# Splitting the flag's step: the minimum on VectorE first, TensorE's matmul four tiles later

## The chip, the cores and the metric

The kernel runs on one core of one Trainium2 chip. Its time is device time in microseconds (us). Three runs of the kernel before took 269.99, 271.73 and 272.43 us, so the median is 271.73; the execution in the profile took 270.14 us, of which the span from the first to the last instruction is 268.4 us.

## What is computed

Four batches of N = 12416 rows of C = 128 numbers go through two attention steps with m = 32 inducing rows, and then through a gated layer of width 1536:

```python
def mab(q, kv):
    s = scale * (q @ kv.transpose(0, 2, 1))
    s = s - s.max(-1, keepdims=True)
    a = np.exp(s)
    a /= a.sum(-1, keepdims=True) + 1e-09
    return a @ kv
h = mab(I, x)          # 32 rows look at all of x
y = mab(x, h)          # all of x looks at the 32 rows
...
gate = np.maximum(y @ w_gate, 0.0)
val = y @ w_val
out = (gate * val) @ w_out
```

The result has 49664 rows of 128 numbers in float32.

## The kernel before

Since every row of y is a weighted mean of the same 32 rows h, gate and val are weighted means of 32 rows too, once it is known which of the gates are positive. For each batch the kernel builds a table of the products of pairs of these rows, multiplied with w_out; each output row is then a sum over pairs, with an exponential of a sum of two scores for each pair. This holds if, for each of the 1536 units, the sign of the gate is the same for all rows. The kernel bounds that from the scores it has seen. Per batch, `certain` (L432) puts what it finds into `kept` (128 x 12) and `near` (128 x 1), by a few small operations on VectorE and GpSimd. After the last batch, `flag` (L806) takes the smallest of them: a minimum over the columns of `kept` (L809), a minimum with `near` (L810), a matmul with a matrix of ones which adds up the 128 partitions on TensorE (L812), a comparison (L814) and a cast to an integer (L818). The result `left` is loaded into a register by all engines (L885), and only if it is positive a second, general kernel runs after this one. With these inputs it does not run.

The rest of the work around the flag is the output of the last batch. A batch has 97 tiles of 128 rows, numbered 0 to 96. `scores` (L558) makes a buffer of exponentials: TensorE adds pairs of scores into one of two PSUM buffers `e_ps` (L569), and ACT takes the exponential into one of 20 buffers `F` (L576). `outputs` (L583) makes one tile: four matmuls with the table (L591) and a fifth (L593) into a third of a PSUM buffer `o_ps`. There are two such buffers. After three tiles `outputs_end` (L599) lets VectorE take the reciprocal of the row sums (L607) and multiply (L608) into an output buffer; after six tiles that is sent to memory by the sync queue (L617).

Nothing is scheduled automatically. The order of instructions on every engine is the order in which the Python code emits them, and that is written by hand in the string `ORDER`: each letter is a step. E is one call of `scores`, O is one tile, and s, x, p, u, l and t take the next step of a list ("lane"). The lane s has, per batch, the scores of the next pieces of x and then the three steps of the bound; the last entry is the flag. Each engine takes its own instructions in that order and waits where an input or a buffer isn't ready.

At the end of the string the last s is the flag, behind tile 77 of the last batch. Tile 77 is the third of its group (75, 76, 77). After it stand tile 78, the last E of full size, tiles 79 to 89, the E of the last 128 columns, tiles 90 to 95, x and tile 96. The value load L885 stands after tile 88.

Of the kernel before, what the change touches and what calls it, by code (L numbers as in the profile page):

```python
# [10 lines left out]
FP32 = mybir.dt.float32  # L11
FP16 = mybir.dt.float16
AF = mybir.ActivationFunctionType
ALU = mybir.AluOpType
AX = mybir.AxisListType


def quadratic_kernel(tc, x, inducing, moe_w_gate, moe_w_val, moe_w_out, out):


    with ExitStack() as ctx:
        return quadratic_body(
            ctx, tc, x, inducing, moe_w_gate, moe_w_val, moe_w_out, out
        )


def quadratic_body(ctx, tc, x, inducing, moe_w_gate, moe_w_val, moe_w_out, out):
    nc = tc.nc
# [3 lines left out]
    P = 128  # L32
# [20 lines left out]
    def st(shape, dtype, tag, bufs, name=None, pool=None):  # L53
        return (pool or sb).tile(shape, dtype, tag=tag, bufs=bufs, name=name or tag)
# [13 lines left out]
    ones32 = constp.tile([P, P], FP32, name="ones32")  # L68
    ones16 = constp.tile([P, P], FP16, name="ones16")
    zero16 = constp.tile([1, 2 * P], FP16, name="zero16")  # L70
    kept = constp.tile([P, NFF], FP32, name="kept")
    near = constp.tile([P, 1], FP32, name="near")
# [40 lines left out]
    def mt(shape, dtype, tag, bufs, name=None):  # L113
        return st(shape, dtype, tag, bufs, name, pool=mp)
# [216 lines left out]
    def bank(tag, name, shape, dtype=FP32):  # L331
        return psum.tile(shape, dtype, tag=tag, bufs=2, name=name)
# [8 lines left out]
    dve, act, pool = nc.vector, nc.scalar, nc.gpsimd  # L341
# [318 lines left out]
    lanes = {"p": [], "u": [], "s": [], "x": [], "l": [], "t": []}  # L660
    turning = []

    def plan_scores(b):
        for q in range(0 if b else 1, NCH):
            lanes["s"].append(lambda q=q: pair_out(b, q, *pair_scores(b, q)))
            lanes["x"].append(lambda q=q: pair_exp(b, q))
        lanes["s"] += [
            lambda: bound1(b),
            lambda: (bound2(b), bound3(b)),
            lambda: certain(b),  # L670
        ]

    def plan_phase1(b):

        s = state[b]
# [127 lines left out]
        for n, g in late[::-1]:  # L803
            todo.insert(n, g)
        lanes["u"] += todo
    def flag():  # L806

        sure = mt([P, 1], FP32, "v", 1)
        dve.tensor_reduce(out=sure, in_=kept, axis=AX.X, op=ALU.min)  # L809
        dve.tensor_tensor(out=sure, in0=sure, in1=near, op=ALU.min)  # L810
        ps = bank("m", "flag_ps", [P, 1])
        nc.tensor.matmul(ps, ones32, sure, start=True, stop=True)  # L812
        f32 = mt([P, 1], FP32, "eps", 1)
        dve.tensor_scalar(  # L814
            out=f32, in0=ps, scalar1=P - 0.5, scalar2=1.0, op0=ALU.is_le, op1=ALU.mult
        )
        left = flag.left = constp.tile([P, 1], mybir.dt.int32, name="left")
        dve.tensor_copy(out=left, in_=f32)  # L818

    lanes["u"].append(lambda: gate_sum(0, 1))  # L820
    for b in range(1, B):
        plan_phase1(b)
    for b in range(B):
        plan_scores(b)
    lanes["s"].append(flag)


    def all_k(t0, nt):
# [70 lines left out]
    "OOEOOsEEOOpOOEOpEOOOuEOuuEOOEOOuEOEuOOxOOsEEOxOOOOuuEEOsOOOEuuOOEOuOExOOOuOuEEOOxsOuEsEs"  # L899
    "uOOOOEOEuuEOuOEsEEOOOOuOEEOOuuOsEOOEOuuEEOOOEOOuOEuOEuOOOuOOxEEOOOuOEEOOOOOOEEOOOOEOOOxO"  # L900
    "EEOOOOsEOEOxOOOEEOOOOEOOEOOEsEOOEOOOEsEOOxOOOEEOOOEOOOEOOExOOOOEEsOOOEOOOEsOOOEEOsOOOxsO"
    "EEOOOOEOOOOEEOOOsOEOOOOOOOOOOOEOOOOOOxO"
)


# [202 lines left out]
```

The softmax here doesn't subtract the row's maximum and nothing guards it: scores larger than these inputs give would overflow.

## Time and profile before

| what | value |
|---|---|
| median of three runs | 271.73 us |
| profiled execution, span | 268.4 us |
| TensorE busy (matmul) | 247.3 us, 92% |
| ACT busy | 227.5 us, 85% |
| VectorE busy | 214.3 us, 80% |
| GpSimd busy | 27.1 us, 10% |
| mean granted TensorE clock | 0.986 |
| HBM read and written | 27.80 and 25.43 MB |

Busy times are sums over the whole span, and several engines can be busy at once. What sets the time is read from the chain that ended last, which is followed back from the last instruction, and from the waits: who stood idle, until whose result came. In the tables of the trace, a name such as `o_ps` is the program's name of a buffer, "L591" is the line of the code, "PE" is TensorE, "PEld" its weight loads, "DVE" VectorE, "ACT" ScalarE, "POOL" GpSimd and "SP" the sync engine, which issues the output transfers. The last operation of VectorE ends at 262.56 us, and the last output transfer is issued at 262.60 us.

### The profile page before, as it was taken

What the parts mean: (1) busy time and instruction counts of PE and PEld (TensorE: products, weight loads), DVE (VectorE), ACT (ScalarE), POOL (GpSimd) and SP (SyncE); (2) the same over time, 40 slices, a digit from 0 to 9 for tenths busy, and PEclk for the clock granted to TensorE, in tenths of its full rate; (3) what the DMA queues carried; (4) which work ended last, traced back from release to release, by engine and by line L of the source; (5) the groups of instructions that cost most, each with busy time, mean ns of one, the idle gap of its engine ahead of it and who ended that gap; (6) DMA issues with size and microseconds to landing.
All of it is one profiled execution on the core that took longest, in us unless ns stands there. A gap on an engine that the chain in (4) does not pass through costs nothing.

```text
span 268.4 us, 9193 instructions
## 1 busy us (share of the span) xinstructions
PE 247.3 (92%) x3885; PEld 186.6 (70%) x3885; DVE 214.3 (80%) x584; ACT 227.5 (85%) x305; POOL 27.1 (10%) x71
## 2 busy tenths in 40 slices
PE   2996899999999999998899999999999999999890
PEld 0794677777667776876787778666776786677680
DVE  3576978777899997878998997799999967666761
ACT  4234789999999998998899999989999989999820
POOL 8474000210003002100002000000000000000000
PEclk9999799999999999999999999999999999999997
DMA  7999998999999997997999795232333334234333
GB/s 180 202 206 203 214 191 105 250 194 261 233 193 258 246 172 236 183 264 230 193 249 253 152 197 208 117 120 118 120 120 117 121 131 178 117 120 158 138 152 107
DMA packets 48736, 48.36 MB, mean 180 GB/s; under 512 B 35472, under 2 KB 36656, under 8 KB 48688
## 3 DMA queue, kind: packets, MB, share of 16 engines
q1 hardware_dynamic: 41520, 33.74, 43.8%
q0 software_dynamic: 6880, 13.50, 28.5%
q8 instruction: 32, 0.52, 0.8%
q10 hardware_dynamic: 288, 0.46, 0.5%
q14 instruction: 16, 0.13, 0.1%
HBM read 27.80 MB, written 25.43 MB: 198 GB/s over the span
## 4 chain that ended last, share of the span: by engine, by line
PE 71%; DVE 15%; ACT 9%; issue 3%; POOL 0%; ACTq 0%; DVEq 0%; POOLq 0%
PE o_ps L591 30%; PE e_ps L569 14%; ACT F L576 7%; PE o_ps L593 6%; DVE osb L608 4%; DVE U L473 3%; PE T_ps L519 3%; PE s_ps L707 2%; PE s_ps L372 2%; PE T_ps L505 2%; PE hz_ps L729 2%; PE xT_ps L262 2%; PE s_ps L273 1%; PE T_ps L539 1%; PE xT_ps L698 1%
## 5 line engine op out<-in xcount | busy, mean ns | idle before, releaser
L576 ACT ACTIVATE F<-e_ps 128x1024 f16<-128x1024 f32 x192 | 185.1, 1027 | 13.1 <-PE e_ps L569 10.9
L591 PE MATMUL o_ps<-T,F 128*128 128x129 f16 x1536 | 129.5, 221 | 3.5 <-DVE osb L608 3.3
L591 PEld LDWEIGHTS <-F 128*128 128x128 f16 x1536 | 98.5, 97 | 30.0 <-issue 21.2
L593 PE MATMUL o_ps<-T,p 128*128 128x129 f16 x388 | 84.5, 218 | 0.0
L608 DVE TENSOR_TENSOR osb<-o_ps,rzo 128x384 f32<-128x384 f32 x132 | 72.5, 549 | 4.5
L569 PE MATMUL e_ps<-sc,sel 32*128 32x512 f16 x384 | 57.3, 386 | 0.5 <-ACT F L576 0.4
L593 PEld LDWEIGHTS <-p 128*128 128x128 f16 x388 | 37.9, 98 | 0.4
L607 DVE RECIPROCAL rzo<-o_ps 128x3 f32<-128x3 f32 x132 | 23.0, 175 | 17.4 <-PE o_ps L593 15.9
L569 PEld LDWEIGHTS <-sel 32*128 32x128 f16 x384 | 15.5, 91 | 17.1 <-issue 3.9
L640 DVE TENSOR_REDUCE reach<-sc 128x1 f32<-128x512 f16 (+1 forms) x28 | 17.6, 627 | 1.0
L628 DVE TENSOR_SCALAR sc<-s_ps 128x512 f16<-128x512 f32 (+1 forms) x28 | 17.5, 627 | 0.9 <-PE s_ps L372 0.8
L655 ACT ACTIVATE p<-sc 128x512 f16<-128x512 f16 (+1 forms) x28 | 16.4, 586 | 0.0
L275 ACT ACTIVATE p<-s_ps 128x256 f16<-128x256 f32 (+3 forms) x16 | 5.3, 333 | 10.8 <-PE s_ps L273 10.8
L263 DVE COPY xT<-xT_ps 128x1024 f16<-128x1024 f16 (+2 forms) x15 | 8.7, 584 | 4.2 <-PE xT_ps L262 2.7
L709 ACT ACTIVATE p<-s_ps 128x512 f16<-128x512 f32 (+1 forms) x21 | 11.4, 551 | 0.2
L442 POOL TENSOR_SCALAR ok<-eps 128x1 f32<-128x1 f32 x4 | 0.9, 234 | 104.3 <-DVE rzo L607 104.3
L482 DVE TENSOR_TENSOR U<-U,U 128x1536 f16<-128x1536 f16 (+1 forms) x12 | 10.8, 899 | 0.0
L707 PE MATMUL s_ps<-indT,xT 128*128 128x32 f16 x288 | 10.0, 177 | 0.2 <-ACT F L576 0.2
L519 PE MATMUL T_ps<-wo,U 128*128 128x128 f16 x144 | 10.0, 219 | 0.1
L86 POOL DMA_DIRECT2D x<-in_x_dram x18 | 9.7, 550 | 1.1 <-issue 1.0
L707 PEld LDWEIGHTS <-xT 128*128 128x128 f16 x288 | 8.9, 96 | 0.9 <-DMA xT<-x 0.5
L372 PE MATMUL s_ps<-xT,h 128*32 128x512 f16 x96 | 9.5, 388 | 0.0
(160 smaller groups left out, 249.1 us busy)
## 6 DMA issues: line engine op xcount, KB each, us to landing
out_dram<-osb SPq DMA_DIRECT2D x64, 384.0 KB, 3.3
x<-in_x_dram POOLq DMA_DIRECT2D x18, 512.0 KB, 10.9
x<-in_x_dram POOLq DMA_DIRECT2D x8, 256.0 KB, 7.9
x<-in_x_dram POOLq DMA_DIRECT2D x5, 128.0 KB, 8.0
osb<-in_x_dram ACTq DMA_DIRECT2D x1, 384.0 KB, 4.4
osb<-in_x_dram SPq DMA_DIRECT2D x1, 384.0 KB, 4.2
wg<-in_moe_w_gate_dram POOLq DMA_DIRECT2D x1, 384.0 KB, 8.0
wv<-in_moe_w_val_dram POOLq DMA_DIRECT2D x1, 384.0 KB, 9.0
```

The costliest lines, as they stand in the source:

```text
L372: nc.tensor.matmul(ps[32 * r : 32 * r + 32, 0:w], state[b]["h2"], xTs(state[b]["xT"], (4 * q + r) * TPB, w // P), start=True, stop=True,)
L519: nc.tensor.matmul(ps, u_cols(0, t, j), wo[:, t, :], start=t == 0, stop=t == NFF - 1)
L569: nc.tensor.matmul(ps[:, r, :], sel4[rows, j, :], sc[rows, :], start=True, stop=True)
L576: act.activation(out=F[b, q, d, j], in_=ps, func=AF.Exp, scale=sm_scale2)
L591: nc.tensor.matmul(ps, f, T[b % 2][:, j, 0 : P + 1], start=j == 0, stop=False)
L593: nc.tensor.matmul(ps, p2s[b, q][rows, tok], T[b % 2][rows, 4 + r, 0 : P + 1], start=False, stop=True)
L607: dve.reciprocal(out=rz[:, 0:k, :], in_=outputs.ps[:, 0:k, P : P + 1])
L608: dve.tensor_tensor(out=osb[:, a6 : a6 + k, :], in0=outputs.ps[:, 0:k, 0:P], in1=rz[:, 0:k, :].broadcast_to([P, k, P]), op=ALU.mult,)
L628: dve.tensor_scalar(out=scs[b, q][0:k, 0:w], in0=ps[0:k, 0:w], scalar1=64.0, scalar2=-64.0, op0=ALU.min, op1=ALU.max,)
L640: dve.tensor_reduce(out=state[b]["reach"][0:k, q : q + 1], in_=scs[b, q][0:k, 0:w], axis=AX.X, op=ALU.max, apply_absolute_value=True,)
L655: act.activation(out=p2s[b, q][0:k, 0:w], in_=scs[b, q][0:k, 0:w], func=AF.Exp, scale=sm_scale2)
L707: nc.tensor.matmul(ps[:, t, :], s["xT"][q][:, t, :], indT, start=True, stop=True)
```

## The change

The flag's step is cut in two. The first, `worst`, holds the two minimum operations on VectorE. The second keeps the name `flag` and holds the matmul, the comparison and the cast. The first stands where the whole step stood, behind tile 77; the second stands behind tile 81, four tiles and one E later. The purpose is that TensorE can go on with tiles while VectorE makes the matmul's input. The operations and their data stay the same.

```diff
-    def flag():
-
-        sure = mt([P, 1], FP32, "v", 1)
+    def worst():
+        flag.sure = sure = mt([P, 1], FP32, "v", 1)
         dve.tensor_reduce(out=sure, in_=kept, axis=AX.X, op=ALU.min)
         dve.tensor_tensor(out=sure, in0=sure, in1=near, op=ALU.min)
+
+    def flag():
+
         ps = bank("m", "flag_ps", [P, 1])
-        nc.tensor.matmul(ps, ones32, sure, start=True, stop=True)
+        nc.tensor.matmul(ps, ones32, flag.sure, start=True, stop=True)
...
-    lanes["s"].append(flag)
+    lanes["s"] += [worst, flag]
...
-    "EEOOOOEOOOOEEOOOsOEOOOOOOOOOOOEOOOOOOxO"
+    "EEOOOOEOOOOEEOOOsOEOOOsOOOOOOOOEOOOOOOxO"
```

## The prediction

> **What bounds the kernel now.** I read the page first: busy shares, then the chain that ended last.
>
> ```profile
> PE 247.3 (92%) x3885; PEld 186.6 (70%) x3885; DVE 214.3 (80%) x584; ACT 227.5 (85%) x305; POOL 27.1 (10%) x71
> ...
> PE 71%; DVE 15%; ACT 9%; issue 3%; POOL 0%; ACTq 0%; DVEq 0%; POOLq 0%
> ```
>
> TensorE carries 71% of the chain: any stretch in which it stands still is lost unless something later makes it wait anyway. So I asked for the waits of the last 29 us, where the flag is:
>
> ```profile
> DVE rzo L607 <- PE o_ps L593: 5.4, 10, 1.0
> ...
> PE flag_ps L812 <- DVE v L810: 1.1, 1, 1.1
> ...
> DVE eps L814 <- PE flag_ps L812: 0.5, 1, 0.5
> ```
>
> The columns are total us, times, longest. VectorE waits for tiles there ten times and 5.4 us, so it has room; TensorE waits 1.1 us once, at the flag's matmul. The chain around it (start, length, what) shows why:
>
> ```profile
> 253.51 0.07 PE o_ps L593
> 253.58 0.02 issue
> 253.60 0.19 DVE rzo L607
> 253.79 0.02 issue
> 253.81 0.56 DVE osb L608
> 254.37 0.08 DVE v L809
> 254.45 0.02 issue
> 254.48 0.17 DVE v L810
> 254.65 0.04 issue
> 254.69 0.38 PE flag_ps L812 x2
> 255.07 0.26 PE o_ps L591 x4
> ...
> 256.97 0.23 PE o_ps L591 x4
> 257.21 0.07 PE o_ps L593
> 257.28 0.39 PE o_ps L591 x4
> 257.67 0.06 PE o_ps L593
> ```
>
> The flag's matmul is queued straight behind tile 77, the last of its group of three. VectorE can reach the flag's minimum only after that group's reciprocal and product, so TensorE pays for all of it: from 253.58, when tile 77 ends, to 255.07, when tile 78 starts, 1.49 us, of which 1.11 us are waiting and 0.38 us the flag's matmul. Tile 84 takes 0.45 us (257.28 to 257.73) where its neighbours take 0.29: the timeline puts a wait of 0.17 us for the product L608 ahead of its weight load, a free o_ps buffer. ACT is not the limit here either:
>
> ```profile
> 252.53 1.94 ACT L576 ACTIVATE F<-e_ps 128x1024 f16<-128x1024 f32 x2 [0.39 <-PE e_ps L569]
> 255.81 1.03 ACT L576 ACTIVATE F<-e_ps 128x1024 f16<-128x1024 f32 x1 [1.34 <-PE e_ps L569]
> ```
>
> It idles 1.34 us behind the same stall, since the scores that feed it stand behind the flag.
>
> **What the skill says.** "TensorE: Matmul & The Clock Gate", the section on the array of 32×32 sub-arrays, says that TensorE's queue may pull weight loads ahead of matmuls in flight, while ACT and DVE are strict FIFO. The trace agrees: no o_ps weight load starts between 253.29 and 254.82, so nothing useful passes the waiting flag, and VectorE's minimum starts only after L608. "Perfetto Trace Analysis", Matmuls, wants independent groups to rotate through PSUM banks, so that evacuation overlaps the next matmuls: with two o_ps buffers tile 78 could run beside the evacuation of tiles 75 to 77, and only the flag keeps it out. "DMA: Bandwidth & Descriptors", Latency and other measured facts, gives a floor of about 600 ns for a tensor_load; the five loads of the flag's value took 467 to 820 ns, so the trace decides.
>
> **The change part by part.** No instruction is added or removed; VectorE's two small operations (0.15 and 0.16 us) keep their place, while the matmul, the comparison and the cast move. In the changed program TensorE has tiles 78, scores, 79, 80, 81, then the flag's matmul, then 82. VectorE has the minimum, then the group 78 to 80, then comparison and cast, then 81 to 83, 84 to 86, the value load.
>
> 1. The wait at tile 77. Tile 78 needs the buffer of group 72 to 74, evacuated at 252.92 (L608, 252.36 + 0.56), so it starts at 253.58. With the slots of the chain (78: 0.31; scores and 79: 0.72; 80 and 81: 0.29 each) 81 ends at 253.58 + 1.61 = 255.19. Its inputs are there: the scores need an e_ps buffer, free when the first of the two ACT pieces ends at 253.50; tile 80 needs the F that the second gives at 254.47, and starts at 254.61.
> 2. The flag's matmul at 255.19. Its input is ready at 254.64, so a margin of 0.55 us, and no wait. Its cost inside a running stream is not shown: at most the present 0.38 us; the nearest row is the bound's matmul L395, also two fp32 passes, with 0.28 us in the chain. I take 0.28, so tile 82 starts at 255.19 + 0.28 = 255.47. Before, the chain has tile 78 at 255.07, the scores at 255.38, and tiles 79 to 82 at 255.71, 256.10, 256.39 and 256.68. So tile 82 moves from 256.68 to 255.47: **−1.21 us** (1.11 of waiting and 0.10 of a cheaper slot; with a slot of 0.38 it is −1.11).
> 3. The wait of 0.17 us at tile 84. Tiles 82 and 83 take 0.60 us (256.68 to 257.28), so 84 starts at 256.07. Its buffer is that of group 78 to 80: end of tile 80 at 254.90, reciprocal, product of 0.56 us, done at about 255.70. No wait: 0.45 − 0.29 = **−0.16 us** more.
> 4. Comparison and cast on VectorE, 0.16 and 0.15 us: they follow the product at 255.70 and the matmul at 255.47, and end at about 256.05; the next group's last tile ends at 256.07, so they cost nothing.
> 5. The new wait that matters is for the flag's value, ready at about 256.05 rather than 255.45. TensorE's sequencer loads it now at 258.2, ahead of tile 89; moved by 1.37 us it asks at 256.8, 0.8 us after it is ready. ACT's load comes after its last F (then 254.5 to 255.5) and has until the next scores, 259.18 − 1.37 = 257.8. VectorE's load takes 0.82 us and now holds L607 from about 259.2, when tile 89's group is complete, to 259.48; nobody waits, as the buffer is free at 260.25 and wanted at 260.48. The same order remains, so the same slack.
> 6. The end. VectorE's last product ends at 262.56, the last output's DMA is issued at 262.60, and the span ends at 268.4. The output DMAs of the tail land in 2.3 to 3.3 us each and their queue waits for VectorE (L608: 11.5 us in five waits), so the transfers follow the tiles and the end moves with them.
>
> Sum: −1.21 − 0.16 = −1.37 us, that is 0.5% of 271.73: **270.4 us**.
>
> **The rivals.** (a) *Hidden end.* If the transfers or the last waits, not the tiles, set the end, the gain vanishes: 271.7. For it: 5.8 us lie between the last product and the end. Against: the queue waits for VectorE rather than VectorE for it.
> (b) *Part is given back.* The flag's value comes 0.6 us later on the clock and is wanted 1.37 us earlier, so its slack on TensorE shrinks from 2.8 to 0.8 us; or VectorE falls behind with the four small operations. A loss of half gives 271.0. Against: VectorE is busy 5.1 of 7.5 us from 255.07 on.
> (c) *Slower.* The flag's value misses the sequencers: if comparison and cast slipped behind another whole group (0.9 us), the value would come at 256.9, and a load of 0.5 us on TensorE and then 0.8 us on VectorE before the group of tile 89 would stand in the path, with a restart behind them. With the gain used up and 0.5 + 0.8 + 0.9 = 2.2 us on top of 271.7, that is 273.9. The VectorE order (comparison ahead of group 81 to 83) speaks against it.
> (d) *More than the count.* The three times are 269.99, 271.73 and 272.43, the profiled run 270.14. If the executions at 272 have longer stalls at such hand-overs than the profiled one, or the median of before was a high draw, the new time is near 270.14 − 1.37 = 268.8.
>
> **How the numbers follow.** The count: 0.60; (a) 0.07; (b) 0.10; (c) 0.05; (d) 0.18. The predicted time is the count's, 270.4. The spread of single executions, 2.4 us, is larger than the effect and makes most of the range: downward it takes in (d), 268.4; upward it takes in (a) and (b), 271.8; (c) stays out. A change over 1% needs 2.7 us, twice the count. Faster by that comes from (d) and the lucky tail of the count: 0.25. Slower comes from (c) and an unlucky median under (a): 0.07. Within 1%: 0.68.
>
> **What would show it.** In the changed profile, TensorE's wait for the flag's input should be gone from the waits, or under 0.1 us; between the end of tile 77 and the start of tile 78 nothing; the last F on ACT follows the others with no idle of 1.3 us; tile 84 takes 0.29 us; the flag's matmul adds about 0.28 us between 81 and 82 (step 2). A TensorE gap near the value load would be (b) or (c). From the end of tile 77 to VectorE's last product, 8.98 us now, should be 7.6 us. I am wrong if that stretch shrinks and the time doesn't, or if a wait for VectorE appears at the moved matmul.

## The result and the profile after

The changed kernel takes 269.62 us (median of 18 runs, 268.12 to 271.13), the kernel before 271.5 us (18 runs, 269.99 to 272.43): ratio 0.9943, 95% interval 0.9923 to 0.9963. That is 1.5 us less, between 1.0 and 2.1; the ratio is that of the means, and the two medians alone lie 1.9 us apart. The span of the profiled execution fell from 268.4 to 267.1 us.

The busy time of TensorE is unchanged; the chain's share of "issue" and of ACT is a little lower. This is the page of the changed kernel:

```profile
PE 247.3 (93%) x3885; PEld 186.7 (70%) x3885; DVE 214.4 (80%) x584; ACT 227.3 (85%) x305; POOL 27.1 (10%) x71
...
PE 71%; DVE 16%; ACT 8%; issue 2%; POOL 0%; ACTq 0%; DVEq 0%; POOLq 0%
```

In these two profiles the same 247.3 us of matmuls stand in a span that is 1.3 us shorter: work was not saved, standing was. (Spans of single profiles scatter by more than that, so this alone would not show a gain.) The waits of the changed kernel from 240 us on (total us, times, longest) no longer hold a line of the flag's matmul. Their last line is:

```profile
...
PEld L591 <- DVE osb L608: 0.2, 1, 0.2
```

It is worth a look: the wait of 0.2 us for a free output buffer, which the prediction expected to go, is still there. The chain of the changed kernel (start, length, what) shows where:

```profile
253.46 0.06 PE o_ps L593
253.52 0.23 PE o_ps L591 x4
...
255.10 0.17 PE flag_ps L814 x2
255.28 0.26 PE o_ps L591 x4
...
255.88 0.23 PE o_ps L591 x4
...
256.17 0.23 PE o_ps L591 x4
...
256.76 0.39 PE o_ps L591 x4
257.15 0.06 PE o_ps L593
```

Tile 77 ends at 253.52 and tile 78 starts at once. The flag's matmul lies between tiles 81 and 82 and takes 0.17 us of the chain, where it took 0.38. Tile 84 (255.88 to 256.17) now takes 0.29 us; but tile 87 takes 0.45 (256.76 to 257.21). ACT runs the last three exponentials of full size without a gap between them, where the last of them had waited 1.34 us:

```profile
252.48 2.85 ACT L576 ACTIVATE F<-e_ps 128x1024 f16<-128x1024 f32 x3 [0.39 <-PE e_ps L569]
```

Single executions scatter by 3 us, more than the effect, so the experiments are compared by one stretch of the profile, the **tail**: from the start of tile 77's last matmul (L593) to the end of VectorE's last product (L608). Its two ends (start, length; the first from the timeline, the second from the chain) are, before:

```profile
253.34 0.22 PE L593 MATMUL o_ps<-T,p 128*128 128x129 f16 x1
...
262.27 0.29 DVE osb L608
```

and after:

```profile
253.30 0.22 PE L593 MATMUL o_ps<-T,p 128*128 128x129 f16 x1
...
260.88 0.29 DVE osb L608
```

So it is 262.56 − 253.34 = **9.22 us** before and 261.17 − 253.30 = **7.87 us** after. The "stretch" of the expectations was counted from the end of tile 77 in the chain, but for the run with the later load, which already uses the tail. To a stretch 0.24 us is to be added (8.98 is 9.22; in the changed kernel it is 0.22, so such sums hold to about 0.02 us).

### The profile page after: what moved, and what is told of

The parts are those of the page before. It is cut to its first block, busy times and chain, and to the rows that moved or that the text cites. A ratio compares the mean times of both kernels' runs of the same rounds, so it can differ in the third digit from the quotient of the medians.

```text
span 267.1 us, 9193 instructions
## 1 busy us (share of the span) xinstructions
PE 247.3 (93%) x3885; PEld 186.7 (70%) x3885; DVE 214.4 (80%) x584; ACT 227.3 (85%) x305; POOL 27.1 (10%) x71
## 4 chain that ended last, share of the span: by engine, by line
PE 71%; DVE 16%; ACT 8%; issue 2%; POOL 0%; ACTq 0%; DVEq 0%; POOLq 0%
PE o_ps L591 30%; PE e_ps L569 14%; PE o_ps L593 6%; ACT F L576 6%; DVE osb L608 4%; DVE U L473 3%; PE T_ps L519 3%; PE s_ps L707 2%; PE xT_ps L262 2%; PE s_ps L372 2%; PE T_ps L505 2%; PE hz_ps L729 2%; PE s_ps L273 1%; PE T_ps L539 1%; PE xT_ps L698 1%
## 5 line engine op out<-in xcount | busy, mean ns | idle before, releaser
L593 PE MATMUL o_ps<-T,p 128*128 128x129 f16 x388 | 84.5, 218 | 0.0
L608 DVE TENSOR_TENSOR osb<-o_ps,rzo 128x384 f32<-128x384 f32 x132 | 72.5, 549 | 4.5
L593 PEld LDWEIGHTS <-p 128*128 128x128 f16 x388 | 38.0, 98 | 0.4
L505 PE MATMUL T_ps<-won,U 128*128 128x128 f16 x96 | 7.1, 239 | 2.6 <-DVE U L473 2.5
```

The source lines that it names most:

```text
L593: nc.tensor.matmul(ps, p2s[b, q][rows, tok], T[b % 2][rows, 4 + r, 0 : P + 1], start=False, stop=True)
L608: dve.tensor_tensor(out=osb[:, a6 : a6 + k, :], in0=outputs.ps[:, 0:k, 0:P], in1=rz[:, 0:k, :].broadcast_to([P, k, P]), op=ALU.mult,)
```

## The experiments

Each ratio is to runs of the kernel before that were made beside it.

| kernel | minimum behind tile | matmul behind tile | tail, us | ratio to before (95%) |
|---|---|---|---|---|
| before | 77 | 77 | 9.22 | 1 |
| both halves in place | 77 | 77 | 9.21 | 0.9998 (0.9976 to 1.0021) |
| one tile later | 77 | 78 | 8.90 | 0.9991 (0.9971 to 1.0012) |
| two tiles later | 77 | 79 | 8.21 | 0.9982 (0.9961 to 1.0002) |
| changed kernel | 77 | 81 | 7.87 | 0.9943 (0.9923 to 0.9963) |
| minimum earlier | 74 | 77 | 7.86 | 0.9950 (0.9929 to 0.9971) |
| six tiles later | 77 | 83 | 7.83 | 0.9948 (0.9930 to 0.9967) |
| six later, load later | 77 | 83 | 7.93 | 0.9933 (0.9908 to 0.9958) |
| ten tiles later | 77 | 87 | 8.94 | 0.9995 (0.9974 to 1.0015) |
| no flag | none | none | 7.68 | 0.9938 (0.9915 to 0.9961) |

All of them are the changed kernel with another place for the letters s in the last piece of `ORDER`, but for the last and the one with the later load.

**Both halves in place.** The cut alone, with no move:

```diff
-    "EEOOOOEOOOOEEOOOsOEOOOsOOOOOOOOEOOOOOOxO"
+    "EEOOOOEOOOOEEOOOssOEOOOOOOOOOOOEOOOOOOxO"
```

> The step is cut in two, but both halves stand behind tile 77, where the whole step stood. Theory W (the 1.11 us wait for the minimum is what the change removes): every engine has the instruction order of the kernel before, so TensorE's wait for the minimum is back at 1.1 us, the stretch from the end of tile 77 to the last product of VectorE takes 8.98 us as before (7.65 in the changed kernel), ratio to before 1.000. Rival S (the measured ratio of 0.994 is mostly a matter of the build or of scatter): the ratio stays near 0.994.

The tail is 9.21 us, the ratio 0.9998, and the wait is back, in the waits of this kernel from 250 us on:

```profile
PE flag_ps L814 <- DVE v L809: 1.1, 1, 1.1
```

So the gain is neither the build nor scatter.

**Minimum earlier.** The other half of the change instead: the matmul stays where it was, and the minimum goes three tiles ahead.

```diff
-    "EEOOOOEOOOOEEOOOsOEOOOsOOOOOOOOEOOOOOOxO"
+    "EEOOOOEOOOOEEsOOOsOEOOOOOOOOOOOEOOOOOOxO"
```

> The matmul stands behind tile 77 as before, but the minimum stands behind tile 74, one group of tiles earlier. Theory W: no wait for the minimum, since it is done at about 253.3 and TensorE arrives at 253.6; the matmul's slot falls to about 0.18 us, so the stretch is 8.98 - 1.11 - 0.20 = 7.67 us and the ratio 0.994 to 0.995. The wait for a free output buffer stays at tile 84 and does not appear at tile 87. Rival M (the gain is from moving the matmul to another place in TensorE's stream, as ACT's scores pass ahead of it): with the matmul in its old place most of the gain is gone, stretch above 8.5 us, ratio 0.998 or more.

The tail is 7.86 us (expected 7.67 + 0.24 = 7.91). TensorE's matmuls in this kernel's timeline (start, length; tile 77's last, the flag's pair, tile 78's first four) show no wait:

```profile
255.72 0.22 PE L593 MATMUL o_ps<-T,p 128*128 128x129 f16 x1
255.77 0.33 PE L814 MATMUL flag_ps<-v,ones 128*128 128x1 f32 x2
255.97 0.40 PE L591 MATMUL o_ps<-T,F 128*128 128x129 f16 x4
```

The buffer wait is at tile 84 (0.46 us from the last matmul of the tile before to its own, where 0.29 is usual) and not at 87, as expected. The gain therefore comes from the distance between minimum and matmul, whichever of the two is moved; the rival that the matmul's new place brings it is out.

**One and two tiles later.** Here the distance is shorter than the wait.

```diff
-    "EEOOOOEOOOOEEOOOsOEOOOsOOOOOOOOEOOOOOOxO"
+    "EEOOOOEOOOOEEOOOsOsEOOOOOOOOOOOEOOOOOOxO"     (behind 78)
+    "EEOOOOEOOOOEEOOOsOEOsOOOOOOOOOOEOOOOOOxO"     (behind 79)
```

> The minimum behind tile 77, the matmul one tile later, behind tile 78. Theory W: the input comes at the same time, about 254.6, and TensorE arrives 0.31 us later than in the kernel before, so the wait is 1.11 - 0.31 = 0.80 us and the stretch 8.98 - 0.31 = 8.67 us; ratio 0.998 to 1.000. Rival M (any move of the matmul out of its place brings the gain): the stretch is near 7.7 us.

> The matmul two tiles and one scores step after the minimum, behind tile 79. Theory W: tiles 78 and 79 and the scores take 0.31 + 0.72 = 1.03 us, so the wait is 1.11 - 1.03, at most 0.1 us; the matmul no longer lies between tiles 80 and 84, so the buffer wait is at tile 84 and not at 87. Stretch 8.98 - 1.03 - 0.18 = 7.75 us or a little less, ratio 0.994 to 0.996. A wait of more than 0.2 us would be against W.

Behind tile 78 the wait shrinks by what one tile covers, and the tail is 8.90 us where 8.67 + 0.24 = 8.91 was expected:

```profile
256.19 0.38 PE L814 MATMUL flag_ps<-v,ones 128*128 128x1 f32 x2 [0.84 <-DVE v L809]
```

Behind tile 79 I expected 7.75 + 0.24 = 7.99 and measured 8.21: a miss. In this kernel's timeline tile 79's last matmul starts at 254.46 and the flag's at 254.80, 0.34 us later, where next work follows in 0.06; and the pair takes 0.38 us of the chain, the same as before the change. The weight load of the flag's matmul waited too:

```profile
PEld flag_ps L814 <- DVE v L809: 0.3, 1, 0.3
```

So here it did not run beside the last matmul of tile 79, as it does with that of tile 81 in the changed kernel (both start at 254.89). The 0.17 to 0.18 us were seen only where the matmul did not wait. The ratio, 0.9982, is above the expected 0.994 to 0.996 as well; the 1.01 us by which the tail is shorter would be 0.9963, inside its interval.

**Six tiles later.** The buffer wait, now at tile 87, should go if the matmul lies in both intervals.

```diff
-    "EEOOOOEOOOOEEOOOsOEOOOsOOOOOOOOEOOOOOOxO"
+    "EEOOOOEOOOOEEOOOsOEOOOOOsOOOOOOEOOOOOOxO"
```

> The matmul stands two tiles later still, behind tile 83. Theory W, with the buffer wait counted: from the end of a group to the first tile of the group after next TensorE needs about 1.03 us between; three tiles give 0.87. The changed kernel's matmul helps at tile 84 and leaves 0.16 us of waiting at tile 87; here it lies in both intervals (80 to 84 and 83 to 87), so both waits go and the stretch is 7.65 - 0.16 = 7.49 us; the value load has some tenths of a us left and TensorE doesn't stand there. Rival L (the slack of the value load is used up): TensorE stands at tile 88 or 89 and the stretch is 7.65 us or more. Both within 0.1 % in the time: ratio 0.993 to 0.995.

Half came true. No wait for L608 is left, so tiles 84 and 87 have none. But the tail is 7.83 us, not 7.49 + 0.24 = 7.73, since tile 89 takes 0.42 us instead of 0.29. The comparison and cast end at 258.13, and TensorE's load of the value starts at 258.2 and takes 0.49 us:

```profile
L887 PEldq TENSOR_LOAD <-left x1: 486/486/486, 258.2 to 258.2; - x1
```

Tile 89's first matmul starts at 258.68, with the end of that load. In the changed kernel TensorE's load starts about 0.7 us ahead of tile 89 (256.8 against 257.50 in the chain); that would be about 258.0 here (tile 88 ends at 258.71), ahead of the cast's end. It started only after the cast and ended 0.13 us too late for tile 89. The buffer wait was traded for one on the flag's value.

**Six tiles later, load later.** The load is moved too, from tile 88 to tile 90:

```diff
-            if g == B * NSLOT - 3 and t % TPB == 0:
+            if b == B - 1 and t == 90:
```

> The matmul behind tile 83, and in addition the load of the flag's value two tiles later, behind tile 90 of the last batch. In the run with the matmul behind tile 83 alone, the buffer waits went, but tile 89 took 0.42 us instead of 0.29, as the load was asked for at the moment the value was cast. Theory W with that reading: the load is no longer in the way, tile 89 is back at 0.29 us, no tile waits, and the stretch from the start of tile 77's last matmul to VectorE's last product is 7.83 - 0.13 = 7.70 us (9.22 before, 7.87 in the changed kernel, 7.68 without the flag). Rival D: VectorE's own load of 0.5 to 0.8 us now stands ahead of the products of a later group and delays the end instead; stretch 7.83 us or more. Ratio to before 0.993 to 0.995 either way.

Tile 89 is back at 0.29 us, but the tail is 7.93 us: tile 91 now takes 0.52 us. TensorE's load starts at 258.1, when the value has long been there (cast at 257.25), and takes 0.755 us, to 258.86; tile 91 starts at 258.90:

```profile
L887 PEldq TENSOR_LOAD <-left x1: 755/755/755, 258.1 to 258.1; - x1
```

The expectation failed, and not by the rival that was named (VectorE's load, 0.55 us, delays nothing): it is TensorE's own load, to whose end tile 91 is tied here as tile 89 was before. What makes one such load 0.49 and another 0.76 us stays open. The ratio of 0.9933 overlaps that of all the good versions, so it doesn't show that this one is faster.

**Ten tiles later.** The step in the prediction on the value's slack, tried to the end:

```diff
-    "EEOOOOEOOOOEEOOOsOEOOOsOOOOOOOOEOOOOOOxO"
+    "EEOOOOEOOOOEEOOOsOEOOOOOOOOOsOOEOOOOOOxO"
```

> The matmul ten tiles after the minimum, behind tile 87, one tile ahead of the load of the flag's value. Theory W with the rival of the prediction in which the value comes too late: VectorE compares and casts only after the group of tiles 84 to 86, so the value is ready about 0.7 us after TensorE's matmul, and the load takes 0.5 us more; TensorE stands about 0.8 to 1.1 us at tile 88 or 89, stretch 8.3 to 8.7 us, ratio 0.997 to 0.999. If the loads run beside the tiles at no cost, the stretch is 7.5 to 7.7 us.

The tail is 8.94 us (expected 8.54 to 8.94), and the ratio 0.9995: of the 1.35 us by which the tail had become shorter 0.28 are left, and the time shows no gain. The chain of this kernel passes to VectorE, which reaches the comparison only behind the product of tiles 84 to 86, and then stands for the load:

```profile
259.06 0.56 DVE osb L608
259.62 0.07 DVE eps L816
...
259.71 0.17 DVE left L820
259.88 0.61 issue
260.49 0.39 PE o_ps L591 x4
```

So there is a limit on the other side as well, and rival (c) of the prediction is real: two tiles beyond where the change put the matmul it showed with 0.13 us, and six tiles beyond it takes most of the gain. The places between were not run.

**No flag.** The floor: the four operations are left out and the value is set to zero, so this kernel does not test the signs.

```diff
-        flag.sure = sure = mt([P, 1], FP32, "v", 1)
-        dve.tensor_reduce(out=sure, in_=kept, axis=AX.X, op=ALU.min)
-        dve.tensor_tensor(out=sure, in0=sure, in1=near, op=ALU.min)
+        pass
...
-        ps = bank("m", "flag_ps", [P, 1])
-        nc.tensor.matmul(ps, ones32, flag.sure, start=True, stop=True)
...
-        dve.tensor_copy(out=left, in_=f32)
+        dve.memset(left, 0)
```

> The changed kernel without the minimum, the matmul, the comparison and the cast: the flag's value is set to zero, so the test of the signs is left out. It is the floor for every placing of the step. Theory W: the changed kernel pays only the matmul's slot of 0.18 us, so the stretch is 7.65 - 0.18 = 7.47 us, with one buffer wait of 0.16 us at tile 84; ratio to before 0.993 to 0.995. Rival H (part of the step's cost is still hidden in VectorE or the loads): the stretch is 7.2 us or less.

The tail is 7.68 us (expected 7.47 + 0.24 = 7.71), with one buffer wait at tile 84 (0.17 us; the trace names the setting of the value, L812, which VectorE does right behind the product L608). The whole flag cost 9.22 − 7.68 = 1.54 us before, and 0.19 us after the change: one slot of the matmul.

## Why the prediction was right, step by step

The predicted time was 270.4 us, the measured one 269.62; the count was −1.37 us, the tail shows −1.35, and the ratio −1.5 with an interval that holds both. The mechanism of the main term and the sum are right; two of the terms were off, one by 0.10 and one by 0.16 us, in opposite directions. That the sum still fits within some hundredths is luck. That the time itself is 0.8 us lower than predicted comes to 0.2 us from the median of the kernel before (271.73 in three runs, 271.5 in eighteen); the rest is within the scatter.

1. The wait of 1.11 us at tile 77: gone, as said. The two runs with a shorter distance, and the one that moves the minimum instead, show that it is this wait. The predicted chain ended tile 81 1.61 us after tile 77; it took 1.58. One reading is a little off: the minimum starts at 254.29, 0.08 us before the product L608 ends at 254.37, so VectorE takes it up behind the product but not quite after its end.
2. The flag's matmul: no wait, as said. The slot was mis-sized: I took 0.28 us from the bound's matmul and it takes 0.18 (0.17 in the chain of two kernels). That row has 128 columns to move, this one has 1. Its weight loads start at 254.89, together with tile 81's last matmul, and so run beside it at least in part. Which of the two makes it cheaper than 0.28 no run separates. The term is −1.31 instead of −1.21.
3. The buffer wait at tile 84, −0.16 us: this step failed. It is gone at tile 84, but the prediction did not follow the buffers on to tile 87, where the timeline of the changed kernel has it back:

```profile
256.74 0.23 PEld L591 LDWEIGHTS <-F 128*128 128x128 f16 x4 [0.17 <-DVE osb L608]
```

The three tiles between take 0.87 us, and the buffer of the group before them is free about 0.16 us later than that. In the kernel before, the wait at 84 lies in both intervals, 80 to 84 and 83 to 87, and serves both. After the change the matmul (0.17 us) lies in the first and not in the second, so the second wait appears. Its placing behind tile 83 removes both, and without any flag the wait is back at 84; that part is shown.
4. Comparison and cast: free, as said. The cast ends at 255.87 and the group of tiles 81 to 83 is complete at 255.88.
5. The value's slack: TensorE asked at 256.8, as predicted, 0.9 us after the cast. The run with the matmul six tiles later shows the slack used up, that with ten tiles later what it costs when it is missed; so (c) is real, but did not come at tile 81.
6. The end: it moved with the tiles. From the last product to the end of the span are 5.84 us before and 5.93 after, so rival (a), a hidden end, is out; so is (b) as it was put, since the value's slack and VectorE's order gave nothing back: what came back is the 0.16 us of step 3. Case (d) cannot be told from scatter: 269.62 lies between its 268.8 and the count's 270.4.

## What to carry to other kernels

A small step that goes from one engine to another and back costs little work, but in a hand-written order it can stop the busier engine for all that the other has queued ahead of it. Cut it at the hand-over and put as much work between as covers the other engine's backlog. Here that was 1.11 us: two tiles and one E (1.03 us) were just too few, four tiles and one E (1.58 us) were enough, and three tiles were not tried. Put no more there than that, since what waits for its end moves closer. In this kernel it made no difference to the tail whether the producer was moved ahead (7.86 us) or the consumer back (7.87 us). When a wait for a buffer seems to vanish, follow the same buffers one more round before the gain is booked.

## What the runs showed that was not expected

- A matmul pair that waits takes 0.38 us of the chain, and the same pair in a running stream 0.17 to 0.18 (before, both halves in place, one and two tiles later; against the changed kernel, the earlier minimum, and both kernels with six tiles). A wait of about 0.1 us, behind tile 79, therefore cost 0.3.
- The load of a value into TensorE's registers took 0.48 to 0.49 us in eight of the ten profiles, 0.56 and 0.76 in the others. In the kernel before it starts at 258.2, so it ends at about 258.7, as the next tile begins (258.72). It has next to no room: the one of 0.76 us was 0.27 us longer and cost 0.23 us.
- The scatter of single executions comes at least in part from another place. Between 28 and 34 us the granted TensorE clock was 0.72 in the changed kernel's profile and 0.51 in that of the earlier minimum, and tile 77's last matmul started at 253.30 and 255.72 us, while the tails differ by 0.01 us. In both profiles the lower clock begins around the end of a stand of TensorE of 2.53 us, in which it waits for VectorE's `U` (L473). No run varied that wait, so it stays open whether it is the cause, and what sets the length of the stretch. Over 22 runs of the kernel with the matmul behind tile 83, span and mean clock go together (correlation −0.87; in the other sets of runs −0.59 to −0.92). So spans of single profiles could not be compared here, and the tail could.
